# FFN output products that wait for the quarter of w_out they read, with scores one chunk further ahead

## The chip, the cores and the metric

One core of a Trainium2 chip runs the kernel. The metric is the device time of one execution in microseconds. The page and the trace come from one profiled execution.

## The reference

Talking-heads attention over 8 batches, 12 heads, 448 positions and 64 dimensions a head, then a feed-forward layer with a squared ReLU:

```python
scores = scale * np.matmul(q, k.transpose(0, 1, 3, 2))
scores = np.einsum('bhij,hg->bgij', scores, w_pre)
scores = scores - np.max(scores, axis=-1, keepdims=True)
attn = np.exp(scores)
attn = attn / (np.sum(attn, axis=-1, keepdims=True) + 1e-09)
attn = np.einsum('bhij,hg->bgij', attn, w_post)
out = np.matmul(attn, v)
# transposed to x: 3584 tokens x 768
h = np.maximum(x @ w_in, 0.0)      # w_in: 768 x 2048
result = (h * h) @ w_out           # w_out: 2048 x 768
```

Inputs and output are float32 in memory; the products are taken in bfloat16 with float32 sums.

## The kernel before

**A planner writes the order.** Every piece of work is given to a `Planner` as an operation with an engine (or a choice between DVE and ACT), a duration that the author estimated, a priority, and the operations that it depends on. `run()` plays the engines forward by these estimates: whenever an engine is free it takes the ready operation with the smallest priority. What comes out is one fixed order for each engine, in which the instructions are issued. The planner's dependences therefore decide only the order; on the chip, each instruction waits by semaphores for the data that it really reads and for the buffers that it overwrites, and an engine takes its instructions in order.

**Attention.** Work on a batch runs over 45 chunks of up to 10 query positions with all 12 heads (120 rows, plus 4 rows of padding). The place of a chunk, `n = 45 * b + c`, is the clock that all priorities count in. For a chunk:

- scores q·k for a whole block of positions (L741; four blocks a batch, `C0 = [0, 6, 19, 32]`), evacuated from PSUM to `snat` by DVE or ACT (`copy`, L534 and L536);
- a relayout by a DMA on SP's queue, `snat` to `sch` (`move`, called by `relayout`), so that heads lie on partitions;
- the mix of heads with w_pre on PE (L901, or L847 for two chunks at once on quarters of the array; L907 for the first chunks of batch 0), the row maximum on DVE (L912), the exponential on ACT (L915), the reciprocal on DVE (L922), w_post scaled by it on POOL (L925, tile `wq`);
- the mix with w_post, which also transposes (L932), evacuated into `atb` by DVE or ACT; then, for half a batch at once, the product with v (L978), evacuated into `xt`.

The scores of a block have the priority of the block's first chunk less `AHEAD`, less up to some nine chunks more for the earlier pairs of heads; a relayout has the priority of its chunk less `AHEAD`:

```python
pri = b * NCHUNK + first - AHEAD - 0.6 - (0.7 if r == 0 else 1.4) * (NPAIR - p)   # score
pri = n - AHEAD                                                                    # relayout
```

From batch 2 on, k and q are turned by DMA transposes on SP's queue (`x_piece`, `x_tail`), which stand between the relayouts there.

**FFN.** The tokens of two batches (896) are cut into units of 128 or 256 tokens; there are 17, numbered `ix`. A unit does its up products (L1037, `w1` against `xt`), a ReLU by DVE or ACT (L1051, L1055, tile `hr`), a square on POOL (L1058, tile `h2`), and its output products (L1076, `h2` against `w2`). All FFN products have priorities of a million and more, so PE takes them only where no attention work is ready: they are its filler. An output group is 128 tokens by 384 columns: 16 products over `ft`, planned in eight steps of two (`OSTEP = 2`, `f0 = 0, 2, ..., 14`).

**w_out** comes in four quarters on POOL's DMA queue, issued at steps 14, 17, 20 and 23 of batch 0 (`load_w2`, L1186). Quarter `f4` holds rows `f` from `8 * (f4 % 2)` (in units of 128) and columns from `384 * (f4 // 2)`: 0 and 1 are the first half of the columns, 2 and 3 the second half. `w2_in[f4]` is the planner's mark that it is there.

**Stand-ins.** Up to 130 us of planned time, where the planner finds PE without work and sparsely used, it puts in a product of a zero tile that nobody reads (`stand`, L1301, tile `still`), which keeps PE occupied.

Of the kernel before, what the change touches and what calls it, by code (L numbers as in the profile page):

```python
# [40 lines left out]
PIECE = NPAIR // 2  # L41
NE = 6
NSCH = 14
AHEAD = 7.0
FIFO = 50
IDLE_NS, IDLE_COLS, IDLE_FROM, IDLE_END, IDLE_LOW = 112, 256, 1300, 130000, 0.62
SPELL, PHASE, DROP, RISE = 3413, 1700, 0.4, 0.8
# [9 lines left out]
OSTEP = 2  # L57
# [28 lines left out]
SOON = 0  # L86
# [42 lines left out]
class Planner:  # L129
# [8 lines left out]
    def add(self, eng, ns, pri, fn, deps=(), lat=60, bank=None, frees=None, mode=0):  # L138
        op = Op(eng if isinstance(eng, dict) else {eng: ns}, lat, pri, fn, list(deps), bank, frees, mode)
        self.ops.append(op)  # L140
        return op
# [199 lines left out]
def kernel(  # L341
# [190 lines left out]
    def copy(eng, out_, in_):  # L532
        if eng == "DVE":
            nc.vector.tensor_copy(out=out_, in_=in_)  # L534
        else:
            nc.scalar.copy(out=out_, in_=in_)  # L536
# [4 lines left out]
    add = pl.add  # L541
    FILL = 1e6
    slots = {}
# [12 lines left out]
    def keep(key, fn):  # L556
        def go(*got):
            for key_, slot in zip(key if isinstance(key, list) else [key], got):
                slots[key_] = slot
            fn(*got)  # L560
        return go
# [12 lines left out]
    h_op, sq_op, o_op, st_op = {}, {}, {}, {}  # L574
# [137 lines left out]
    def place_of(b, c):  # L712
        return b * NCHUNK + (ORDER0.index(c) if b == 0 else c)
# [6 lines left out]
    def is_direct(b, c):  # L720
        return b == 0 and C0[1] <= c <= C0[2]
# [5 lines left out]
    def score(b, r, group):  # L727
# [17 lines left out]
        first = min(place_of(b, c) for c in range(C0[r], (C0 + [NCHUNK])[r + 1]) if not is_direct(b, c)) - b * NCHUNK  # L745
        pri = b * NCHUNK + first - AHEAD - 0.6 - (0.7 if r == 0 else 1.4) * (NPAIR - p)
        n = b * (NJ + 1) + r - 2
# [30 lines left out]
    def relayout(b, c):  # L778
# [6 lines left out]
        deps = list(scopy[b, r]) + (list(scopy[b, r - 1]) if r == 1 and cc == 0 else [])  # L785
        pri = n - AHEAD
        if r == 2 and cc == 0:
# [15 lines left out]
        else:  # L803
            o = cc - 1
            if b >= PAIR_FROM:
                pri = n - o % (2 * PAIRS) + 0.1 * (o % (2 * PAIRS)) - AHEAD
            o, step = (2 * CI * (o // 2) + o % 2, 2) if b >= PAIR_FROM else (o, CPR)
# [207 lines left out]
    def units_of(pair):  # L1015
        return UNITS if pair else UNITS0
# [3 lines left out]
    def unit(pair, ui):  # L1020
        a, z = units_of(pair)[ui]
        w = z - a
        nf = 512 // w
        ix = len(units)
        units.append((pair, ui))
        h2_ = h2[ix % 2]
        fill = FILL + 100 * ix
        xdeps = [op for t0, t1, op in xc_op[pair] if t0 < z and t1 > a]
        old_o = o_op.get(ix - 2, [])
        h_op[pair, a], sq_op[ix], o_op[ix] = [], [], []  # L1030
        prev = None
        for f0 in range(0, FT, nf):
            key = ("f", ix, "h", f0)
            for j in range(nf):
                def mms(slot, f0=f0, j=j):
                    for c2 in range(NPAIR):
                        nc.tensor.matmul(  # L1037
                            slot[:, j * w:(j + 1) * w], lhsT=w1[c2][:, (f0 + j) * 128:(f0 + j + 1) * 128],
                            rhs=xt[:, c2, a:z], start=(c2 == 0), stop=(c2 == NPAIR - 1),
                        )  # L1040
                if j == 0:
                    prev = add("PE", w * 2.55, fill + f0, keep(key, mms), xdeps + w1_in + [prev], lat=0, bank=key)
                else:
                    prev = add("PE", w * 2.55, 0, lambda key=key, mms=mms: mms(slots[key]), [prev], lat=0)
                h_op[pair, a].append(prev)
            end = add("WAIT%s" % str(key), 0, 0, lambda: None, [prev], lat=200)
            gi = len(hr_log)

            def relu(eng, key=key, gi=gi):
                if eng == "DVE":  # L1050
                    nc.vector.tensor_scalar(  # L1051
                        out=hr[gi % 2][:, :], in0=slots[key][:, :], scalar1=0.0, scalar2=0.0, op0=ALU.max, op1=ALU.add,
                    )
                else:
                    nc.scalar.activation(out=hr[gi % 2][:, :], in_=slots[key][:, :], func=ACT.Relu)  # L1055

            def square(gi=gi, f0=f0):
                nc.gpsimd.tensor_tensor(  # L1058
                    out=h2_[:, f0:f0 + nf, 0:w],
                    in0=hr[gi % 2][:, :].rearrange("p (f c) -> p f c", f=nf),  # L1060
                    in1=hr[gi % 2][:, :].rearrange("p (f c) -> p f c", f=nf), op=ALU.mult,
                )

            rl = add({"ACT": 500, "DVE": 590}, 0, 0, relu, [end, hr_log[gi - 2] if gi >= 2 else None], lat=100, frees=key)
            sq = add("POOL", 1020, FILL, square, [rl] + old_o, lat=70)
            hr_log.append(sq)
            sq_op[ix].append(sq)
        for mt in range(w // 128):
            whole = not (z == W2B and mt == 1 and pair == B // 2 - 1)
            cuts = [0, 384, DMODEL] if whole else [0, 384, 640, DMODEL]  # L1070
            for nt, (c0, c1) in enumerate(zip(cuts, cuts[1:])):
                key = ("f", ix, "o", mt, nt)
                for f0 in range(0, FT, OSTEP):
                    def mms(slot, f0=f0, mt=mt, c0=c0, c1=c1):
                        for ft in range(f0, f0 + OSTEP):
                            nc.tensor.matmul(  # L1076
                                slot[:, 0:c1 - c0], lhsT=h2_[:, ft, mt * 128:(mt + 1) * 128],
                                rhs=w2[:, ft, c0:c1],
                                start=(ft == 0), stop=(ft == FT - 1),
                            )  # L1080
                    if f0 == 0:
                        prev = add("PE", (12 + (c1 - c0) * 5 // 3) * OSTEP / 4, fill + 20 + 4 * mt + 2 * nt, keep(key, mms),
                                   [prev] + sq_op[ix][0:max(1, OSTEP // nf)] + w2_in[0:1 if ix < SOON else 4], lat=0, bank=key)
                    else:
                        prev = add("PE", (12 + (c1 - c0) * 5 // 3) * OSTEP / 4, FILL, lambda key=key, mms=mms: mms(slots[key]), [prev, w2_in[f0 // 4]] + sq_op[ix][0:(f0 + OSTEP + nf - 1) // nf], lat=0)
                    o_op[ix].append(prev)
                end = add("WAIT%s" % str(key), 0, 0, lambda: None, [prev], lat=200)
                si = ix_store[0]

                def evac(eng, key=key, si=si, c0=c0, c1=c1):  # L1090
                    copy(eng, osb[si % 2][:, c0:c1], slots[key][:, 0:c1 - c0])

                ev = add({"DVE": 80 + (c1 - c0) * 25 // 24, "ACT": 165 + (c1 - c0) * 5 // 7}, 0, 0, evac, [end, st_op.get(si - 2)] + ([m_op[n_] for n_ in direct] if si < 2 else []), lat=100, frees=key)
                evs = evs + [ev] if nt == 1 and whole else [ev]
                if nt == 1 or not whole:
                    done = []
                    for rows, dst, o in pieces(pair, a + mt * 128, None if whole else (c0, c1)):
                        side_ = not whole and rows <= CI
                        def store(dst=dst, o=o, rows=rows, si=si, e0=0 if whole else c0, e1=DMODEL if whole else c1, eng=nc.scalar if side_ else nc.gpsimd if whole else nc.sync):
                            eng.dma_start(out=dst, in_=osb[si % 2][o:o + rows, e0:e1])  # L1100
                        done.append(add("ACT" if side_ else "POOL" if whole else "SP", 510 if rows <= CI else 830 if whole else 930, FILL, store, evs))
                    for op in done:
                        op.store = whole
                    st_op[si] = pl.moved("LOAD" if whole else "DMA", 64, 16, 16, 0, done, 700)
            if whole:
                ix_store[0] += 1
# [70 lines left out]
    w2_in = [add("W2", 0, 0, lambda: None, lat=0) for i in range(4)]  # L1177
# [32 lines left out]
    def first_batch():  # L1210
# [35 lines left out]
        for gs in ONE:  # L1246
            av(0, 1, gs, P_ROWS, XB)
        unit(0, 2)

    def next_batch(b):  # L1250
# [91 lines left out]
```

## Time and profile before

| | |
|---|---|
| median of 3 runs | 571.62 us (571.61 to 571.78) |
| the profiled execution | 571.9 us, its span 570.1 us |
| PE busy | 561.1 us, 6340 products |
| DVE, ACT, POOL busy | 500.8, 446.4, 363.0 us |
| stand-in products (L1301) | 50 |
| output products (L1076) | 912, the first at 82.85 us |
| mean granted clock of PE | 0.999 |

The page gives busy time by engine, a strip of 40 slices of the span with busy shares in tenths, the chain of work that ended last, and groups of instructions by source line. Products on PE are pipelined, so the duration of one (323 ns for L1076) is longer than the distance between the starts of two. Times within the span count from its start.

### The profile page before, as it was taken

Reading aid. Unit: us, or ns where it says so; the run is one execution under the profiler, and the core shown is the slowest. Engines: PE = TensorE matmul, PEld = TensorE weight load, DVE = VectorE, ACT = ScalarE, POOL = GpSimd, SP = SyncE. Lnnn points to the kernel's source line nnn. Section 1 sums busy time; section 2 is a strip of 40 time slices with the busy share of each in tenths; the row PEclk is TensorE's granted clock in tenths of the full one; section 3 lists DMA queues with packets and bytes.
Section 4 is the critical chain, followed back from the end, with each engine's and each line's share of the span. In section 5 each row is a group of like instructions: output and inputs, shape, how many; then the busy total and the mean of one; then the engine's idle time right before and its main releaser. Section 6 shows DMA issues by size and latency. Waiting matters only on the chain.

```text
span 570.1 us, 17924 instructions
## 1 busy us (share of the span) xinstructions
PE 561.1 (98%) x6340; PEld 398.5 (70%) x6340; DVE 500.8 (88%) x1109; ACT 446.4 (78%) x1186; POOL 363.0 (64%) x677
## 2 busy tenths in 40 slices
PE   8999999999999999999999999999999999999997
PEld 5667765776677767677667677767667677767785
DVE  7999999999999899989888899998899998998542
ACT  5789988788788888888887888987888878888400
POOL 8667346776677448857578456957569554736451
PEclk9999999999999999999999999999999999999999
DMA  9999859974896739964797739975399656542011
GB/s 136 210 177 223 162 122 184 189 146 111 154 208 120 166 101 178 189 149 113 125 213 122 166 101 160 195 163 138 65 208 171 143 139 113 119 103 79 1 56 55
DMA packets 129949, 80.85 MB, mean 142 GB/s; under 512 B 59274, under 2 KB 126588, under 8 KB 129860
## 3 DMA queue, kind: packets, MB, share of 16 engines
q1 hardware_dynamic: 80756, 46.29, 37.0%
q0 software_dynamic: 49104, 33.43, 36.2%
q8 instruction: 49, 0.80, 0.6%
q14 instruction: 40, 0.33, 0.2%
HBM read 45.61 MB, written 11.01 MB: 99 GB/s over the span
## 4 chain that ended last, share of the span: by engine, by line
PE 90%; DVE 6%; POOL 1%; DMA 1%; issue 1%; ACT 0%; DVEq 0%; POOLq 0%; ACTq 0%
PE bank L1076 27%; PE bank L1037 25%; PE bank L932 13%; PE bank L741 7%; PE bank L978 7%; PE bank L847 5%; PE bank L901 3%; PE bank L907 2%; DVE mn L912 1%; DVE snat L534 1%; DMA sch<-snat 1%; DVE atb L534 1%; PE bank L1301 1%; DVE hr L1051 1%; DVE osb L890 1%
## 5 line engine op out<-in xcount | busy, mean ns | idle before, releaser
L915 ACT ACTIVATE es<-bank,mn 124x448 bf16<-124x448 f32 (+1 forms) x360 | 228.1, 642 | 42.9 <-DVE mn L912 35.8
L912 DVE TENSOR_REDUCE mn<-bank 124x1 f32<-124x448 f32 (+1 forms) x360 | 209.4, 613 | 3.9 <-PE bank L847 3.4
L1076 PE MATMUL bank<-w,h 128*128 128x384 bf16 (+2 forms) x912 | 177.3, 323 | 0.2
L1037 PE MATMUL bank<-xt,w 128*128 128x256 bf16 (+1 forms) x1632 | 164.1, 254 | 0.6 <-DVE hr L1051 0.3
L1037 PEld LDWEIGHTS <-w 128*128 128x128 bf16 x1632 | 132.8, 98 | 25.8 <-issue 12.2
L925 POOL TENSOR_SCALAR wq<-wback_two,rc 124x120 bf16<-124x120 f32 x252 | 88.8, 362 | 86.3 <-DVE rc L922 60.2
L1058 POOL TENSOR_TENSOR h<-hr 128x512 bf16<-128x512 f32 x112 | 115.7, 1037 | 33.1 <-DVE hr L1051 15.1
L932 PEld LDWEIGHTS <-es 124*112 124x112 bf16 (+2 forms) x1440 | 108.0, 129 | 32.5 <-issue 8.8
L534 DVE CAST atb<-bank 112x480 bf16<-112x480 f32 (+3 forms) x196 | 119.1, 617 | 10.6 <-PE bank L932 9.6
L932 PE MATMUL bank<-wq,es 124*112 124x120 bf16 (+2 forms) x1440 | 120.2, 217 | 2.0 <-POOL wq L925 1.5
L1076 PEld LDWEIGHTS <-h 128*128 128x128 bf16 x912 | 80.2, 98 | 55.0 <-issue 16.1
L536 ACT CAST atb<-bank 112x480 bf16<-112x480 f32 (+3 forms) x187 | 98.2, 539 | 16.1 <-PE bank L932 14.5
L536 ACT CAST snat<-bank 128x448 bf16<-128x448 f32 x168 | 84.6, 543 | 11.4 <-PE bank L741 10.6
L534 DVE CAST snat<-bank 128x448 bf16<-128x448 f32 x150 | 89.8, 614 | 0.8 <-PE bank L741 0.3
L1051 DVE TENSOR_SCALAR hr<-bank 128x512 f32<-128x512 f32 x82 | 56.6, 690 | 21.1 <-PE bank L1037 15.7
L915 ACT ACTIVATION_READ_ACCUMULATOR es<-bank,mn 124x1 f32 (+1 forms) x360 | 75.0, 208 | 0.0
L925 POOL TENSOR_SCALAR wq<-wback,rc 124x120 bf16<-124x120 f32 (+1 forms) x94 | 33.6, 365 | 39.3 <-DVE rc L922 26.1
L741 PE MATMUL bank<-kt,qz 64*64 64x448 bf16 (+1 forms) x528 | 44.6, 361 | 0.1
L847 PE MATMUL bank<-sch,wmix 64*64 64x448 bf16 x504 | 42.7, 363 | 0.0
L978 PE MATMUL bank<-atb,vs 112*64 112x192 bf16 (+3 forms) x864 | 40.4, 250 | 0.2 <-DVE atb L534 0.2
L978 PEld LDWEIGHTS <-vs 112*64 112x64 bf16 x864 | 36.5, 110 | 5.0 <-issue 4.5
L1100 POOL DMA_DIRECT2D out_dram<-osb x33 | 19.9, 604 | 29.9 <-DVE osb L534 16.4
(80 smaller groups left out, 397.7 us busy)
## 6 DMA issues: line engine op xcount, KB each, us to landing
sch<-snat SPq DMA_DIRECT2D x318, 105.0 KB
out_dram<-osb POOLq DMA_DIRECT2D x21, 384.0 KB, 3.8
vs<-in_v_dram POOLq DMA_DIRECT2D x16, 336.0 KB, 7.8
ks<-in_k_dram POOLq DMA_DIRECT2D x14, 336.0 KB, 8.0
qs<-in_q_dram POOLq DMA_DIRECT2D x14, 288.0 KB, 8.4
w<-in_moe_w_in_dram POOLq DMA_DIRECT2D x6, 512.0 KB, 13.0
w<-in_moe_w_out_dram POOLq DMA_DIRECT2D x4, 768.0 KB, 21.1
out_dram<-osb POOLq DMA_DIRECT2D x8, 192.0 KB, 7.5
```

Of the source, the lines that this page charges most:

```text
L534: nc.vector.tensor_copy(out=out_, in_=in_)
L536: nc.scalar.copy(out=out_, in_=in_)
L741: nc.tensor.matmul(slot[m0:m1, 0:S], lhsT=lhsT[:, m0:m1], rhs=kt[i][half, :, at_, :], start=True, stop=True,)
L847: nc.tensor.matmul(got[i + x][o0:o1, 0:S], lhsT=w[k0:k1, c0:c0 + o1 - o0], rhs=srcs[i + y][k0:k1, :], start=True, stop=True,)
L912: nc.vector.tensor_reduce(out=mn[i][0:rows, :], in_=slots[mk][0:rows, 0:S], axis=AX.X, op=ALU.min)
L915: nc.scalar.activation(out=es[i][0:rows, 0:S], in_=slots[mk][0:rows, 0:S], func=ACT.Exp, scale=-1.0, bias=mn[i][0:rows, 0:1], accum_out=sm ...
L925: nc.gpsimd.tensor_scalar(out=wq[i][0:rows, :, 0:ns], in0=back[0:rows, :, 0:ns], scalar1=rc[i // 2][0:rows, i % 2:i % 2 + 1], scalar2=1.0, ...
L932: nc.tensor.matmul(slot[0:P_KEYS, jb * H * ns:(jb + 1) * H * ns], lhsT=es[i][0:rows, jb * P_KEYS:(jb + 1) * P_KEYS], rhs=wq[i][0:rows, :, ...
L978: nc.tensor.matmul(v_[64 * hh:64 * hh + 64, i, 0:x1 - x0], lhsT=vs[:, 2 * c2 + hh, jb, :], rhs=atb[half][:, jb, 2 * c2 + hh, x0:x1], start ...
L1037: nc.tensor.matmul(slot[:, j * w:(j + 1) * w], lhsT=w1[c2][:, (f0 + j) * 128:(f0 + j + 1) * 128], rhs=xt[:, c2, a:z], start=(c2 == 0), sto ...
L1058: nc.gpsimd.tensor_tensor(out=h2_[:, f0:f0 + nf, 0:w], in0=hr[gi % 2][:, :].rearrange("p (f c) -> p f c", f=nf), in1=hr[gi % 2][:, :].rear ...
L1076: nc.tensor.matmul(slot[:, 0:c1 - c0], lhsT=h2_[:, ft, mt * 128:(mt + 1) * 128], rhs=w2[:, ft, c0:c1], start=(ft == 0), stop=(ft == FT - 1),)
```

## The change

One constant and the dependences of the output products. A group's first step no longer depends on all four marks, but on the mark of the quarter with its first rows and its columns; a later step depends on the quarter that it reads (`2 * (c0 // 384) + f0 // 8`) in place of `f0 // 4`. `AHEAD` goes from 7 to 8, which moves the priority of all scores and relayouts by one chunk. Nothing is computed in another way; the planner makes a new order for every engine from it.

```diff
-AHEAD = 7.0
+AHEAD = 8.0
...
                     if f0 == 0:
                         prev = add("PE", (12 + (c1 - c0) * 5 // 3) * OSTEP / 4, fill + 20 + 4 * mt + 2 * nt, keep(key, mms),
-                                   [prev] + sq_op[ix][0:max(1, OSTEP // nf)] + w2_in[0:1 if ix < SOON else 4], lat=0, bank=key)
+                                   [prev, w2_in[2 * (c0 // 384)]] + sq_op[ix][0:max(1, OSTEP // nf)], lat=0, bank=key)
                     else:
-                        prev = add("PE", (12 + (c1 - c0) * 5 // 3) * OSTEP / 4, FILL, lambda key=key, mms=mms: mms(slots[key]), [prev, w2_in[f0 // 4]] + sq_op[ix][0:(f0 + OSTEP + nf - 1) // nf], lat=0)
+                        prev = add("PE", (12 + (c1 - c0) * 5 // 3) * OSTEP / 4, FILL, lambda key=key, mms=mms: mms(slots[key]), [prev, w2_in[2 * (c0 // 384) + f0 // 8]] + sq_op[ix][0:(f0 + OSTEP + nf - 1) // nf], lat=0)
```

`SOON` is 0, so the first step before waits for `w2_in[0:4]` in every unit.

## The prediction

> **What bounds the kernel now.** The profile page first, for which engine sets the end.
>
> ```profile
> span 570.1 us, 17924 instructions
> PE 561.1 (98%) x6340; PEld 398.5 (70%) x6340; DVE 500.8 (88%) x1109; ACT 446.4 (78%) x1186; POOL 363.0 (64%) x677
> ...
> PE   8999999999999999999999999999999999999997
> ...
> DVE  7999999999999899989888899998899998998542
> ...
> PEclk9999999999999999999999999999999999999999
> ...
> PE 90%; DVE 6%; POOL 1%; DMA 1%; issue 1%; ACT 0%; DVEq 0%; POOLq 0%; ACTq 0%
> ```
>
> PE is busy in all slices and makes 90% of the chain that ended last; the clock granted is full. So the time is PE's own work plus what PE loses. A busy PE need not be useful, though: the timeline of PE, around the time at which the FFN output products begin, shows a hole.
>
> ```profile
> 76.18 0.80 PE L932 MATMUL bank<-wq,es 124*112 124x120 bf16 x8
> 76.81 0.73 PE L901 MATMUL bank<-sch,wmix 124*128 124x448 bf16 x3
> 77.38 1.91 PE L1301 MATMUL bank<-still 128*128 128x256 bf16 x16
> 80.41 0.37 PE L932 MATMUL bank<-wq,es 124*112 124x120 bf16 x4 [1.12 <-POOL wq L925]
> ...
> 82.85 0.49 PE L1076 MATMUL bank<-w,h 128*128 128x384 bf16 x2
> ```
>
> L1301 is the stand-in product whose result nobody reads. From 77.38 to 80.41 PE does nothing useful: 3.03 us, 1.91 in stand-ins and 1.12 idle. The first output product (L1076) starts only at 82.85. When its weights were there, the tile view of moe_w_out tells:
>
> ```profile
> L1186 POOL DMA_DIRECT2D w<-in_moe_w_out_dram x4: 922/928/939, 40.3 to 51.0; - x4
> DMA to landing us min/median/max: 16.4/21.1/25.1
> ```
>
> Issues at 40.3, 43.3, 48.3 and 51.0; landings by the trace's records at 56.7, 63.5, 70.3 and 76.1. The first quarter lay there for 26 us unread. What else limited PE in that stretch, the table of windows shows (columns: window, length, busy time of PE, PEld, DVE, ACT, POOL, clock, DMA):
>
> ```profile
> 60.00:70.00 10.00, 9.34 (x154) 7.28 (x149) 9.71 (x24) 9.35 (x28) 3.10 (x7) 1.00 0.77 153
> 70.00:77.00 7.00, 6.99 (x104) 5.21 (x102) 6.46 (x14) 6.36 (x16) 5.15 (x10) 1.00 0.68 154
> 77.00:81.00 4.00, 2.88 (x31) 2.17 (x29) 4.00 (x11) 3.12 (x10) 0.70 (x2) 1.00 0.34 76
> ...
> 336.00:346.00 10.00, 10.00 (x99) 6.49 (x91) 9.29 (x21) 9.57 (x25) 3.59 (x9) 1.00 0.35 79
> ```
>
> In 77 to 81 DVE is busy for 4.00 of 4.00: with FFN work exhausted, attention runs at DVE's pace and PE waits. In 336 to 346, in the middle of the kernel, PE is full.
>
> **Prices.** From the starts in the timeline of PE:
>
> ```profile
> 339.03 2.76 PE L1076 MATMUL bank<-w,h 128*128 128x384 bf16 x16
> 341.63 0.38 PE L932 MATMUL bank<-wq,es 124*112 124x120 bf16 x4
> 341.94 0.57 PE L741 MATMUL bank<-kt,qz 64*64 64x448 bf16 x8
> 342.44 0.42 PE L932 MATMUL bank<-wq,es 124*112 124x120 bf16 x4
> 342.69 0.49 PE L1076 MATMUL bank<-w,h 128*128 128x384 bf16 x2
> ```
>
> L1076: (341.63 − 339.03)/16 = 0.162 us each. L932 inside its group: 0.052 each by the trace, so four take 0.21; ahead of the quarter-array L741 they take 0.31, so a change of the array's tiling costs 0.10 at most (0.093 over all such places). A stand-in is 0.109. Priced this way over PE's whole order, the program before has 545.4 us of PE work; the other 24.7 us of the span are PE's start (1.06), its tail after the last product (3.4), the half-speed first microseconds, waits up to about 90 us (some 5), and rounding of the prices.
>
> **The change part by part.**
>
> *The wait for w_out.* Before, the first product of every output group is planned behind all four quarters (w2_in[0:4]); the later index f0 // 4 therefore never matters. After, columns 0 to 383 wait for quarter 0, then 1 from f0 = 8, and columns from 384 for 2 and 3. Only units 0 and 1 can notice, since later units are computed with all quarters landed. In the changed program's order, the first L1076 stands behind 28 chunks of L932 (before: 46). It needs quarter 0 after 28 chunks, 1 after 34, 2 after 41 and 3 after 44; the profile of before finishes those chunks at 58.1, 65.5, 76.3 and 81.4, so the landings leave 1.4, 2.0, 6.0 and 5.3 us. POOL issues the four loads behind the same counts of L925 (16, 18, 22, 24), so the landings should stay. The order holds 33 stand-ins in place of 50, and the run of sixteen at 77.38 is gone: output products stand there. Hole filled: −3.03 us; one more stand-in less: −0.1. Since PE is the bound to the end (27 us of pure FFN close the kernel), what is done early is missing from the end.
>
> *AHEAD 7 to 8.* Scores (L741), their evacuations and the relayouts (L772) get a priority one chunk earlier. Counts do not change: SP has 404 rows in both orders, the same 30 transposes among them, each up to four relayouts earlier or six later; nothing waits on SP that did not before. Seven changes of PE's tiling fewer (354 to 347): 7 × 0.093 = −0.65. Work moves from DVE to ACT: 16 L932 evacuations at 617 ns and 6 of scores at 614 leave DVE, 6 of osb at 548 and 5 relus at 690 come, together with 2 fewer xt some −8 us of DVE's 500.8; ACT gets about as much on its 446.4. Neither bounds the whole, so 0, and a help where DVE is full.
>
> *New tight places.* An order in which a consumer stands too close behind its producer stalls PE. I measured distances in PE work in both orders. From a mix (L847, L901) to the L932 of the same chunk, before has four below the 3.7 us at which the trace stops showing waits (short by 1.4 together; one of them gives the 0.31 us wait at 308.3), after has one (0.2). From an L932 to the next user of its bank or of its result, the shortest harmless distance is 0.95; before is short by 0.4 in all, after by 1.5 (eight places, the worst 0.53 at 47 us of PE work). Banks of mixes: before short by about 1.5 near 31 us of work, after by 0.8 there and 0.9 later. Sums 3.3 and 3.4; without the part of before that lies in the hole (0.5), after is worse by 0.6. Bounds: −2 (the early waits of before do not return) and +7.4 (second rival). I take +0.6, the counted value.
>
> Sum: −3.03 − 0.1 − 0.65 + 0.6 = −3.2 on the profiled execution's 571.9, so 568.7; the median of the runs lies 0.3 below that execution: **568.4**. Anything within 0.2%, 1.1 us, would pass for no change.
>
> The clock: the first seventeen stand-ins start 0.224 us apart, the sixteen at 77.38 run in 1.91 us, 0.119 each, and PEclk is full, so the hole cost no clock. The Trainium skill, "TensorE: Matmul & The Clock Gate", Part 1, speaks against removing stand-ins: it says that PE falls to half rate after an idle window of about 3.4 us. By that rule the sum would stay, because real products replace them; it would matter only in the third rival.
>
> **The rivals.**
>
> *The hole moves.* FFN products done early are missing later. By PE work, the new order has two stretches without any FFN product and with the earlier unit used up: 4.1 us at 101 to 105 (unit 2 done, unit 3 not begun) and 5.4 at 195 to 201 (unit 5 to 6). For it: the table above, where attention alone loses PE time: 60 to 81 us has 19.21 busy, less 1.91 of stand-ins, 17.3 useful of 21, 3.7 us lost. Against it: before has a like stretch, 4.1 us between units 9 and 10 near 346, and PE is 10.00 of 10.00 busy there. If one of the two stretches pays 3.0 to 3.7, the time is 571.4 to 572.1: no change.
>
> *Both stretches starve*, at the price of that early window: +7.4, 568.4 + 7.4 = 575.8. It ends slower than now by over 0.2% once the two together lose more than 3.2 + 1.1 = 4.3 us. Its place is attention at DVE's pace with one chunk more of score evacuations ahead of the row maxima. Against it: DVE has 8 us less to do.
>
> *A quarter lands late.* PE takes its queue in order, so an L1076 waiting for quarter 0 or 1 holds L932 and L901 of the following chunks, and with them POOL, DVE and ACT. Margin 1.4 us; relayouts a chunk earlier share the DMA engines (0.77 busy in 60 to 70). Each us of lateness beyond it costs one us. If a wait of 4 us also put PE back to the pace of its first stand-ins for as long as those lasted (3.81 us, half of it lost), the time is 568.4 + 4.0 + 1.9 = 574.3. Without the clock it needs 4.3 us of wait to be slower.
>
> That the edit does nothing is excluded by the two orders.
>
> **How the numbers follow.** Forecast 0.66, one stretch starves 0.15, both 0.11, late quarter 0.08. Faster 0.67 (the forecast and a sliver of the second), same 0.14, slower 0.19. The forecast's own range is 565.8 (early waits of before gone, −2.6) to 570.4; the range reaches on over the one-stretch case to 573.0.
>
> **What would show it.** Right: 33 stand-ins, none near 77; first L1076 near 59 us with no idle naming the w_out load ahead of it; PE over 9.8 of 10 in 60 to 70 and full from 70 to 90; DVE about 493 busy; span near 566.9. Wrong: PE idle with wq or mn as releaser near 110 to 120 or 210 to 218 us (the stretches), an L1076 waiting for DMA (late quarter), PEclk below 9 in an inner slice, or PE busy unchanged at 561 with the stand-ins gone, which would mean that the prices, not the waits, moved.

## The result: slower by 0.9%, where 0.6% faster was forecast

The changed kernel takes 576.48 us in the median (575.11 to 578.54, five runs) against 571.61 us for the kernel before (571.54 to 571.78): ratio 1.0091, 95% interval 1.0067 to 1.0115. The forecast was 568.4 with a range up to 573.0. The profiled execution took 576.48 us, so it is 4.6 us longer than that of before, and 7.8 us longer than the sum of the prediction. The runs of the changed kernel differ with the clock that they were granted: 575.1 us at a mean of 0.999, 578.5 at 0.994.

The page of the changed kernel, the lines that were shown of before:

```profile
span 574.5 us, 17927 instructions
PE 561.0 (98%) x6323; PEld 396.7 (69%) x6323; DVE 495.4 (86%) x1096; ACT 452.4 (79%) x1199; POOL 365.3 (64%) x677
...
PE   8999999979999999999999999999999999999997
...
PEclk9999999989999999999999999999999999999999
...
PE 85%; DVE 7%; DMA 3%; issue 2%; ACT 2%; POOL 1%; DVEq 0%; POOLq 0%; ACTq 0%
```

In the ninth slice (115 to 129 us) PE is busy for 7 tenths at 8 tenths of its clock, and 3% of the last chain is now DMA, all of it relayouts (`sch<-snat`). PE's busy time has not fallen although 17 stand-ins are gone.

The part of the change that the prediction priced with confidence came out as written. The timeline of PE at the first output products, and at the place of the old hole:

```profile
58.97 0.35 PE L901 MATMUL bank<-sch,wmix 100*128 100x448 bf16 x1
59.41 0.49 PE L1076 MATMUL bank<-w,h 128*128 128x384 bf16 x2
...
77.10 0.49 PE L1076 MATMUL bank<-w,h 128*128 128x384 bf16 x2
77.43 0.38 PE L932 MATMUL bank<-wq,es 124*112 124x120 bf16 x4
77.64 0.93 PE L901 MATMUL bank<-sch,wmix 124*128 124x448 bf16 x4
```

The first L1076 starts at 59.41 (before 82.85) with no wait for its load, and products of FFN stand where stand-ins stood. The four loads landed at 53.1, 59.7, 66.5 and 73.3, 3 to 4 us earlier than in the kernel before, so the margin was wider than the prediction took. The table of windows says the same (columns: window, length, busy time of PE, PEld, DVE, ACT, POOL, clock, DMA), and goes on to where the time went:

```profile
60.00:70.00 10.00, 9.80 (x134) 6.45 (x134) 9.54 (x23) 8.82 (x24) 2.50 (x8) 1.00 0.77 152
70.00:77.00 7.00, 7.00 (x117) 5.57 (x116) 6.61 (x15) 6.14 (x17) 4.04 (x8) 1.00 0.47 126
77.00:81.00 4.00, 4.00 (x47) 3.03 (x47) 4.00 (x10) 3.59 (x10) 1.52 (x3) 1.00 0.13 18
118.00:130.00 12.00, 9.01 (x82) 6.90 (x80) 7.63 (x17) 6.91 (x19) 6.31 (x12) 0.86 0.72 149
...
220.00:240.00 20.00, 19.23 (x217) 14.68 (x213) 19.37 (x43) 17.01 (x45) 18.34 (x30) 1.00 1.14 180
```

From 118 to 130 us PE is busy for 9.01 of 12.00 at a clock of 0.86 (the kernel before: 12.00 of 12.00 at 1.00). The timeline of PE there:

```profile
118.73 1.48 PE L1037 MATMUL bank<-xt,w 128*128 128x256 bf16 x12
120.13 0.35 PE L741 MATMUL bank<-kt,zt 128*128 128x448 bf16 x1
123.47 0.35 PE L901 MATMUL bank<-sch,wmix 124*128 124x448 bf16 x1 [2.99 <-DMA sch<-snat]
123.66 0.54 PE L741 MATMUL bank<-kt,zt 128*128 128x448 bf16 x2
124.04 0.72 PE L932 MATMUL bank<-wq,es 124*112 124x120 bf16 x8
124.56 2.77 PE L1037 MATMUL bank<-xt,w 128*128 128x256 bf16 x12
```

A mix stands 2.99 us idle for its relayout, and behind it the clock is halved: twelve up products take 2.77 us, where twelve took 1.48 just before. PE takes its queue in order, so the up products behind the mix, whose data lay ready, stood too. What stood ahead of the relayout, the issues on SP's queue tell (changed kernel first, then before):

```profile
106.02 2.49 SPq L643 DMA_TRANSPOSE zt<-qt  x1
108.62 4.64 SPq L673 DMA_TRANSPOSE kt<-kn  x1
113.36 4.11 SPq L679 DMA_TRANSPOSE qz<-qn  x1
117.52 12.95 SPq L772 DMA_DIRECT2D sch<-snat  x14
```

```profile
104.93 4.29 SPq L673 DMA_TRANSPOSE kt<-kn  x1
109.34 1.38 SPq L643 DMA_TRANSPOSE zt<-qt  x1
110.81 1.38 SPq L679 DMA_TRANSPOSE qz<-qn  x1
112.24 11.83 SPq L772 DMA_DIRECT2D sch<-snat  x12
```

Three transposes of batch 2 hold SP for 11.24 us (2.49 + 4.64 + 4.11) in place of 7.05, so the relayouts behind them start at 117.52 and not at 112.24. The chain of waits has the one that the mix stood for as 5.00 us of DMA from 118.34. The same `qz` transpose took 1.38 us in one kernel and 4.11 in the other.

**A ledger.** With the prices of the prediction, every product on PE has a start that PE's work alone would give it. What the real start lies behind that is what PE has lost so far. Read at five times, in the two profiled executions (us):

| | PE work | lost 0–60 | 60–100 | 100–200 | 200–240 | 240–end |
|---|---|---|---|---|---|---|
| before | 545.4 | 9.1 | 3.9 | 1.8 | 0.9 | 5.8 |
| changed | 542.9 | 9.7 | 1.5 | 8.2 | 3.2 | 5.7 |
| difference | −2.5 | +0.6 | −2.4 | +6.4 | +2.3 | −0.1 |

The differences add up to +4.3; the span grew by 4.4. The hole and the counted work brought about what was forecast, and 8.7 us came back between 100 and 240 us. Read in steps of 10 us, some 4.8 of these lie at 120 to 130; 0.9 at 150 to 160, where a second mix waits 0.73 us for its relayout (at 159.73); 1.5 at 230 to 240, where both attention and FFN are there and DVE is full; the rest is spread. Work at half pace counts as lost, too: a clock of 0.86 over 12 us is 1.7 us of full pace, within the 4.8.

Two rows of the changed kernel say where the loss at 200 to 240 us is and where it is not:

```profile
205.00:215.00 10.00, 10.00 (x100) 4.88 (x98) 9.62 (x22) 9.29 (x26) 3.36 (x9) 1.00 0.42 91
230.00:234.00 4.00, 3.39 (x37) 2.58 (x36) 4.00 (x9) 3.45 (x11) 3.42 (x6) 1.00 1.46 214
```

From 215.2 to 221.2, between the last output product of FFN unit 5 and the first up product of unit 6, attention is alone on PE. By the same prices that stretch holds 5.4 us of PE work, and 0.6 us is lost in it.

### The profile page after: what moved, and what is told of

Same layout as the page of the kernel before. It is cut to its first block, busy times and chain, and to the rows that moved or that the text cites. A ratio compares the mean times of both kernels' runs of the same rounds, so it can differ in the third digit from the quotient of the medians.

```text
span 574.5 us, 17927 instructions
## 1 busy us (share of the span) xinstructions
PE 561.0 (98%) x6323; PEld 396.7 (69%) x6323; DVE 495.4 (86%) x1096; ACT 452.4 (79%) x1199; POOL 365.3 (64%) x677
## 4 chain that ended last, share of the span: by engine, by line
PE 85%; DVE 7%; DMA 3%; issue 2%; ACT 2%; POOL 1%; DVEq 0%; POOLq 0%; ACTq 0%
PE bank L1037 25%; PE bank L1076 24%; PE bank L932 13%; PE bank L741 7%; PE bank L978 6%; PE bank L847 5%; DMA sch<-snat 3%; PE bank L901 3%; DVE mn L912 2%; ACT es L915 1%; PE bank L907 1%; POOL wq L925 1%; DVE atb L534 1%; DVE hr L1051 1%; PE bank L1301 1%
## 5 line engine op out<-in xcount | busy, mean ns | idle before, releaser
L1076 PE MATMUL bank<-w,h 128*128 128x384 bf16 (+2 forms) x912 | 181.0, 324 | 0.2
L536 ACT CAST atb<-bank 112x480 bf16<-112x480 f32 (+3 forms) x203 | 105.3, 533 | 24.7 <-PE bank L932 23.8
L932 PE MATMUL bank<-wq,es 124*112 124x120 bf16 (+2 forms) x1440 | 122.0, 218 | 1.8 <-POOL wq L925 1.0
L534 DVE CAST atb<-bank 112x480 bf16<-112x480 f32 (+2 forms) x180 | 111.4, 628 | 10.6 <-PE bank L932 9.8
L1076 PEld LDWEIGHTS <-h 128*128 128x128 bf16 x912 | 79.8, 98 | 54.3 <-issue 16.3
L536 ACT CAST snat<-bank 128x448 bf16<-128x448 f32 x174 | 88.2, 545 | 9.9 <-PE bank L741 8.9
L534 DVE CAST snat<-bank 128x448 bf16<-128x448 f32 x144 | 85.7, 613 | 4.3 <-DMA sch<-snat 2.2
L1051 DVE TENSOR_SCALAR hr<-bank 128x512 f32<-128x512 f32 x87 | 59.9, 689 | 23.1 <-PE bank L1037 19.3
L847 PE MATMUL bank<-sch,wmix 64*64 64x448 bf16 x504 | 41.3, 362 | 0.7 <-DMA sch<-snat 0.7
```

The lines of the kernel that those rows point to most:

```text
L847: nc.tensor.matmul(got[i + x][o0:o1, 0:S], lhsT=w[k0:k1, c0:c0 + o1 - o0], rhs=srcs[i + y][k0:k1, :], start=True, stop=True,)
L932: nc.tensor.matmul(slot[0:P_KEYS, jb * H * ns:(jb + 1) * H * ns], lhsT=es[i][0:rows, jb * P_KEYS:(jb + 1) * P_KEYS], rhs=wq[i][0:rows, :, ...
L1076: nc.tensor.matmul(slot[:, 0:c1 - c0], lhsT=h2_[:, ft, mt * 128:(mt + 1) * 128], rhs=w2[:, ft, c0:c1], start=(ft == 0), stop=(ft == FT - 1),)
```

## The experiments

The theories, by the letters that the expectations use: A, the late second half of batch 2 (its k load waits for a later POOL issue, and its transposes and relayouts with it) makes the wait at 120 us; B, `AHEAD = 8` is the harm by itself; C, FFN products done early are missing later; D, the copies `kn`, `qn` on POOL come behind the squares of an FFN unit that now starts earlier; E, any other order of the same work loses, because the planner does not foresee the waits. All ratios are against the kernel before, run on the same chip, with the 95% interval.

### Each half of the change alone

`w2_only` has the new w_out waits and the old constant, `ahead_only` the reverse:

```diff
# w2_only: the changed kernel with
-AHEAD = 8.0
+AHEAD = 7.0
# ahead_only: the kernel before with
-AHEAD = 7.0
+AHEAD = 8.0
```

> The changed kernel with AHEAD back at 7: only the waits for w_out are changed. The changed kernel's trace shows one wait of 3.0 us at 120.1 to 123.5 for a relayout, queued on SP behind three transposes that took 2.5, 4.6 and 4.1 us, while a k load of batch 2 that POOL issued late (behind 62 L925 in place of 53) was landing. In this program the k load stands behind 53 again. Theory A (the late k load and what it holds up costs the time): no wait near 120, and the gains of the prediction appear, 567.5 to 569.5 us. Theory B (AHEAD 8 crowds SP and DVE all along): the same, 567.5 to 569.5, so this run alone does not part A from B. Theory C (FFN products done early leave a stretch without FFN work later, in which attention runs at DVE's pace): 571 to 573 us, with PE below 4.8 of 5 in windows near 215 to 237.

> The kernel before with AHEAD at 8: the waits for w_out stay at all four quarters. The k load stands behind 53 L925. Theory A (late k load): no wait of 3 us near 120, 570 to 572.5 us, with the hole near 77 still there. Theory B (AHEAD 8 crowds SP and DVE): 574 to 577 us. Theory C: about 571.6, since the FFN products start as late as before.

Measured: `w2_only` 572.06 us (571.08 to 575.56), ratio 1.0009 [0.9995, 1.0023]: no change. `ahead_only` 580.24 (579.22 to 581.6), 1.0149 [1.0131, 1.0167]. The constant costs 8.6 us alone and 4.4 on top of the other edit; the w_out waits bring nothing by themselves, though their hole is filled (loss at 60 to 100 us: 1.3). In `w2_only`, 3.7 us more than before are lost at 200 to 240 us, up to 1.7 of them at half pace (the clock of 0.83 in its row for 205 to 215 below). So C's range holds for `w2_only`, with the loss at 207 to 218 and not at 215 to 237; `ahead_only` lies above all three ranges. `ahead_only` loses its time elsewhere than the changed kernel; its PE at 115 us:

```profile
114.97 0.38 PE L847 MATMUL bank<-sch,wmix 64*64 64x448 bf16 x3
117.54 0.90 PE L847 MATMUL bank<-sch,wmix 60*60 60x448 bf16 x5 [2.19 <-issue]
```

Here, too, the mix comes late behind a `kt` transpose on SP (issued at 112.98, the relayout behind it at 115.60), though the profile names no releaser, and here, too, PE runs at half pace after it: 9.0 us are lost at 100 to 200. The clock is 0.51 from 117 to 124 us, and that alone is 3.4 of the 9.0.

### The wait at 120 us

`k_free` takes the late k load out of the planner's limit of seven loads (in the changed kernel it is issued at 107.1 us, before at 92.3); `stand_in` leaves the wait and fills it with 24 stand-ins, which ask for no data, so that the clock stays up:

```diff
# k_free: the changed kernel with
-        if len(loads) >= 7:
+        if len(loads) >= 7 and len(loads) != 25:
# stand_in: the changed kernel with, ahead of the mix of chunk 77,
+            if n == 77:
+                for _ in range(24):
+                    stand(slot, 0)
```

> The changed kernel, both edits, with one planner dependence left out: the second k load of batch 2 no longer waits for the load seven loads before it (a v load that slipped behind an output store). Its issue returns from behind 62 L925 to behind 53. Theory A: the wait at 120 goes with its half-speed clock after it, 570.5 to 572.5 us if only the 4.9 us that PE lost there come back, and a clock of 0.999 in every run. Theory B: still a wait for a relayout near 120, 574 us or more. Theory C: 571 to 573, with the loss near 216 to 237 left.

> The changed kernel with 24 stand-in products (2.6 us) put into PE's queue right ahead of the mix that waits at 120 us; they wait for nothing but their bank. The wait for the relayout stays. If the spread of the changed kernel's runs (575.1 to 578.5, clock 0.999 to 0.994) is PE's clock halved after an idle time of 3 us, every run shows a clock of 0.999 and 574.5 to 575.7 us. If the spread comes from the DMA side (how long the transposes take), it stays as wide, 575 to 578.5.

`k_free`: 577.02 us (576.66 to 578.4), 1.0095 [1.0078, 1.0112]. The wait at 120 is gone (2.1 us lost at 100 to 200, the changed kernel 8.2). That does not prove A: of the second half's transposes that of k is issued no earlier (134.67; in the changed kernel 134.56) and only that of q is (137.50 for 141.46), and the first half's hold SP as long (106.20 to 117.01). So transposes that hold SP until 117 us do not make the wait by themselves; PE has to come to such a mix by then, and in the planner's new order it does not. A's and C's ranges are missed, and B's is met without B's wait. The time is the same, because 5.9 us are lost at 200 to 240 in place of 3.2, with this line of PE's timeline in the middle:

```profile
208.43 0.42 PE L847 MATMUL bank<-sch,wmix 64*64 64x448 bf16 x4
211.54 0.72 PE L932 MATMUL bank<-wq,es 124*112 124x120 bf16 x8 [2.69 <-POOL wq L925]
```

`stand_in`: 575.22 us (574.32 to 576.93), 1.0062 [1.0045, 1.0079]. PE is full and at full clock from 118 to 130:

```profile
118.00:130.00 12.00, 12.00 (x129) 10.04 (x130) 9.23 (x21) 8.88 (x24) 7.64 (x15) 1.00 0.76 151
```

The median falls by 1.3 us and the profiled execution by 2.2, about the 1.7 of half pace; but the runs of the two kernels overlap, so the size is not settled. They were to lie at 574.5 to 575.7 with the clock at 0.999 in every run, and they spread from 574.32 to 576.93 with 0.994 in the slowest: the halved clock at this place is not all of the spread. The wait itself stays, now filled with work that nobody reads. So a busy PE at full clock can still be late.

### The place at 205 to 215 us

FFN unit 5 takes the first 128 tokens of batch 2, which the first half of that batch's attention gives; unit 6 needs the second half. Between them PE has attention alone. Three kernels ask what makes that stretch dear. `w2_half` gives DVE less to do in batch 2 (its row maxima run over 224 of 448 keys: another constant is subtracted before the exponential, and the normalized result stays the same but for rounding); the `near` kernels let the POOL copies go ahead of the FFN squares, with a control on the kernel before:

```diff
# w2_half: w2_only with
-in_=slots[mk][0:rows, 0:S]
+in_=slots[mk][0:rows, 0:S // 2 if b == 2 else S]
# w2_near, before_near, after_near: w2_only, the kernel before, the changed kernel with
-NEAR_LAST = 2e6
+NEAR_LAST = 9e5
```

> The w_out waits alone, with DVE lightened in batch 2 only: the row maximum there is taken over half of the keys (224 of 448), so that L912 falls from 613 to about 390 ns for 45 chunks, 10 us of DVE's time. (A softmax doesn't depend on which constant is subtracted.) The planner knows nothing of it, so the order is the same as in the run with the w_out waits alone. Theory C (attention at DVE's pace starves PE in 205 to 215): the loss of 3.8 us in 200 to 220 falls under 1.5, 568.5 to 570 us. Theory D: less than that, since attention has fallen behind by late scores and not by DVE: 570 to 572 us.

> The w_out waits alone (AHEAD 7), and POOL's copies of k and q (L660) planned ahead of the FFN squares (NEAR_LAST from 2e6 to 9e5, where squares have 1e6). In the run with the w_out waits alone, up products start 7 us earlier than before (115.2 for 122.2), their squares take POOL, and the copies for the second half of batch 2 run at 123 to 135 in place of 118 to 122; its second pair of transposes is issued at 133 and 136 in place of 124 and 126. Theory D (the early FFN products delay batch 2 through POOL, PE spends its FFN work meanwhile, and starves when that is used up, near 207): transposes back near 124 to 127, DVE over 18.5 of 20 in 140 to 160, the gap between units 5 and 6 under 5 us, and 568 to 570 us. Theory C alone (FFN work is missing later whatever POOL does, since attention is held by DVE): the gap stays over 8 us and the time 571 to 573.

> The control to the run with the copies first: the kernel before with the same NEAR_LAST, nothing else. Its copies for batch 2 stand where they stood (behind 72 to 74 L925), so theory D expects 570.5 to 572.5 us, with the hole of 3 us near 77 still there. If the order of the copies were worth something by itself, it would be faster by as much as the run with the w_out waits.

> The changed kernel with the copies first (both edits and NEAR_LAST 9e5). Its copies for the second half of batch 2 move from behind 76 to 86 L925 to behind 74 to 78. Theory D: part of the loss between 130 and 240 us goes; the wait at 120 us, which comes from the first pair of transposes, may stay: 571 to 574 us. Theory B (AHEAD 8 by itself): 575 or more.

`w2_half`: 571.61 us (570.6 to 574.65), 1.0010 [0.9995, 1.0026]; the loss at 200 to 240 falls from 4.6 to 3.4, where C asked for under 1.5 and 568.5 to 570 us. The rows of `w2_only` and of `w2_half`:

```profile
205.00:215.00 10.00, 8.75 (x80) 5.52 (x81) 9.42 (x21) 9.97 (x28) 3.40 (x9) 0.83 0.40 108
```

```profile
205.00:215.00 10.00, 8.65 (x105) 5.87 (x103) 9.51 (x22) 9.97 (x28) 3.41 (x9) 1.00 0.42 112
```

The longest wait for `wq` there is 0.96 us in place of 1.00, and the clock was not halved this time, which alone can be the 1.2 us. So it is not shown that DVE's row maxima are a part of the price; ACT is as good as full (9.97 of 10) in both kernels. `w2_near`: 578.21, 1.0118 [1.0097, 1.014]; `before_near`: 579.97, 1.0138 [1.0115, 1.0161]; `after_near`: 585.46, 1.0239 [1.0214, 1.0265]. In `w2_near` unit 6 follows unit 5 after 0.8 us in place of 10.3 and the loss at 200 to 240 is 1.8; but the control shows that the edit costs 8 us by itself (3.6 us are lost at 440 to 460, where nothing of this change happens). `after_near` loses 9.7 at 100 to 200. D is not settled by these kernels: the gap closes, at a price that hides what closing it is worth, and all three times lie above D's ranges.

`before_6` makes attention later instead of FFN earlier, with the old w_out waits; `w2_75` is the new waits with half the step:

```diff
# before_6: the kernel before with
-AHEAD = 7.0
+AHEAD = 6.0
# w2_75: the changed kernel with
-AHEAD = 8.0
+AHEAD = 7.5
```

> The kernel before with AHEAD = 6.0 in place of 7.0: attention work admitted one mix later, the step of ahead_only in the other direction, w_out waits as they were. Theory B (harm grows with AHEAD): not slower than before, 569 to 572. Theory E (any re-planned order loses): 574 to 580 us, with waits over 1 us at batch starts. Theory F (7.0 is the middle, later attention starves the softmax instead): slower too, but the loss lies where attention is at DVE's pace (DVE over 9.8 of 10 in the slice that grows), not at a relayout or a w_out wait.

> The new w_out waits with AHEAD = 7.5, half of the change's step. Theory B: between 572.06 (7.0) and 576.5 (8.0), near 574, the loss near 117 to 131 us appearing in part. Theory E: anywhere from 571 to 580, not ordered by AHEAD; which waits appear is not a part of those of 8.0. Faster than both, under 571, if an order between the two keeps the 3 us of the hole and meets neither loss.

`before_6`: 579.75 us (579.45 to 580.78), 1.0149 [1.0134, 1.0164], so B's "not slower" is wrong: one mix later costs as much as one earlier. The time is in E's range; F's sign, DVE full where the loss is, is missing (1.61 and 0.99 of 2 us in the windows 212 to 214 and 214 to 216). Its PE loses 4.2 us at 200 to 240, at the same place and for the same releaser as `k_free`, without the w_out edit (and some 5 us more than the kernel before after 240):

```profile
211.91 0.38 PE L741 MATMUL bank<-kt,qz 64*64 64x448 bf16 x4
214.76 0.70 PE L932 MATMUL bank<-wq,es 124*112 124x120 bf16 x8 [2.47 <-POOL wq L925]
```

`w2_75`: 573.9 (572.51 to 574.32), 1.0039 [1.0024, 1.0054], between the two as B asked, but with none of the loss near 120 that B asked for (2.2 us at 100 to 200) and 4.2 at 200 to 240.

### Four variants in three orders

If the order as such decides (E), then a change that means nothing should move the time too. `TURN` is the planner's price for a change of PE's tiling; 92 or 98 ns in place of 95 moves its sum by 1 us and gives another order of the same work:

```diff
-TURN = 95
+TURN = 98     # before_turn, w2_turn, ah_t98, af_t98; and 92 in before_t92, w2_t92, ah_t92, af_t92
```

> The kernel before, w_out waits and AHEAD 7.0 as they were, with one price of the planner moved by 3 ns: TURN, what it reckons for a change of the PE array's tiling, 98 in place of 95. No work is added, removed or allowed earlier; only the planner's sums differ, by 1.0 us over 354 changes, and with them the order it settles on (23,513 lines of PE's order differ; 337 changes of tiling in place of 354, -1.6 us at 0.093 each). Theory E (the order of the kernel before is one that happens to fit the chip, and any other order of the same work meets waits of 1 to 3 us that the planner does not see, at batch starts): 574 to 580 us, a few waits over 1 us at places where the kernel before has none, and the hole near 77 us still there. Theory B (AHEAD 8.0 is itself the harm: attention work admitted one mix earlier) : 570 to 572, no new waits over 1 us.

> The new w_out waits with AHEAD 7.0 and TURN = 98 in place of 95, the same 3 ns as in before_turn. With before_turn it makes a second pair for the w_out edit alone under another order. Theory E: w2_turn stands to before_turn as the 3 us of the hole make it, with a spread of some us: 571 to 579, and its loss is not at w2_only's 207 to 218. Theory C (what FFN work is done early is missing later, whatever the order): about equal to before_turn, a gap between FFN units 5 and 6 of 5 us or more.

> AHEAD 8.0 alone (old w_out waits), TURN 92 in place of 95: another order of the same plan. Theory B (AHEAD 8.0 as such is dear): 577 to 582 us, like ahead_only's 580.24, with several us lost between 100 and 140 us. Theory E (the order decides, not AHEAD): anywhere from 571 to 582, the losses at other places than ahead_only's.

> AHEAD 8.0 alone, TURN 98. Theory B: 577 to 582 us, several us lost between 100 and 140 us. Theory E: anywhere from 571 to 582, other places.

> Both edits (the changed kernel), TURN 92. Theory B with C (AHEAD 8.0 loses near 100 to 140 us, and FFN work done early is missing near 200 to 240 us): 575 to 579, with a loss at both places. Theory E: 571 to 580, waits elsewhere.

> Both edits, TURN 98. Theory B with C: 575 to 579, with a loss at both places. Theory E: 571 to 580, waits elsewhere; under 571 would make it the best version of all and the forecast's 568.4 reachable by order alone.

> The kernel before with TURN 92. Theory C with B (the w_out edit and AHEAD 8.0 lose, not the order): 570 to 573 us as at 95 and 98, the hole near 77 us still there and nothing over 1 us lost at 200 to 240 us. Theory E: anywhere from 571 to 580.

> The new w_out waits with AHEAD 7.0 and TURN 92. Theory C (FFN work done early is missing later): 571 to 578, with 2 to 5 us lost at 200 to 240 us beyond the kernel before's 0.9, as in all other kernels with these waits so far. Theory E: anywhere, from 568.5 (the hole's 3 us kept) to 578, the loss not bound to that place.

Median us, with the ratio's interval for the new ones:

| | TURN 92 | 95 | 98 | mean |
|---|---|---|---|---|
| before | 572.99 [1.0008, 1.005] | 571.6 | 572.73 [1.0016, 1.0055] | 572.4 |
| w_out waits | 575.64 [1.0049, 1.0107] | 572.06 | 577.73 [1.0093, 1.0145] | 575.1 |
| AHEAD 8 | 573.78 [1.0019, 1.0051] | 580.24 | 577.93 [1.0064, 1.0148] | 577.3 |
| both | 579.68 [1.0098, 1.0157] | 576.48 | 582.12 [1.0163, 1.0202] | 579.4 |

And the ledger of each profiled execution, with the time from the last output product of unit 5 to the first up product of unit 6:

| | PE work | 0–60 | 60–100 | 100–200 | 200–240 | 240–end | gap 5 to 6 |
|---|---|---|---|---|---|---|---|
| before 92 | 543.9 | 9.1 | 5.0 | 2.1 | 1.1 | 6.6 | 0.2 |
| before 95 | 545.4 | 9.1 | 3.9 | 1.8 | 0.9 | 5.8 | 0.8 |
| before 98 | 543.8 | 9.1 | 3.3 | 2.5 | 0.8 | 7.9 | 4.3 |
| w_out 92 | 543.0 | 9.1 | 1.1 | 4.7 | 5.6 | 6.3 | 13.3 |
| w_out 95 | 542.2 | 8.8 | 1.3 | 3.4 | 4.6 | 7.3 | 10.3 |
| w_out 98 | 543.6 | 8.9 | 0.6 | 6.5 | 5.3 | 8.3 | 13.2 |
| AHEAD 92 | 543.6 | 10.0 | 3.5 | 2.4 | 1.7 | 7.2 | 5.1 |
| AHEAD 95 | 543.3 | 9.6 | 4.0 | 9.0 | 1.5 | 7.7 | 0.2 |
| AHEAD 98 | 543.8 | 10.3 | 4.5 | 2.2 | 1.5 | 7.4 | 0.5 |
| both 92 | 543.7 | 10.0 | 1.4 | 8.0 | 4.5 | 6.8 | 9.9 |
| both 95 | 542.9 | 9.7 | 1.5 | 8.2 | 3.2 | 5.7 | 5.9 |
| both 98 | 544.0 | 10.1 | 1.7 | 4.4 | 8.3 | 8.4 | 13.1 |

The ledger holds half pace, too: about 1.7 us in before 92 (near 80 us), w_out 95, w_out 98 (near 215) and both 95 (near 125), and 3.4 in AHEAD 95.

Four things follow.

*C holds for the w_out waits, but not for the changed kernel's own order.* The six kernels with the new waits lose 2.8 us less at 60 to 100 on the mean (1.3 against 4.0), and 4.0 more at 200 to 240 (5.2 against 1.2): each of the six above 3.1, each of the six others below 1.8. In five of the six the loss sits in the gap. Counted inside the gap alone, gaps of up to 5.1 us lose at most 0.2 us, and gaps of 9.1 to 13.6 lose 2.4 to 5.4 (`w2_half`, `w2_75`, `k_free` and `before_6` among them, the last with the old waits). The changed kernel is the exception, with `stand_in`, which has its order: 0.6 lost in a gap of 5.9, and 1.4 of its 3.2 at 230 to 234. What a long gap is like, the windows 205 to 215 tell, of before (at 95) and of the w_out waits at 92:

```profile
205.00:215.00 10.00, 10.00 (x109) 6.74 (x109) 9.47 (x21) 9.16 (x26) 3.13 (x9) 1.00 0.38 87
```

```profile
205.00:215.00 10.00, 7.15 (x69) 3.88 (x67) 10.00 (x24) 9.52 (x29) 3.49 (x10) 1.00 0.56 162
```

In this kernel it looks like the hole of 77 us again, DVE busy for all of 10.00 and PE waiting, only later. In others it is not DVE that is full: in `w2_only` and `w2_half` it is ACT. So what is common is that attention alone does not fill PE; which engine holds it is not shown. And PE's timeline in the second kernel has the line that the prediction had set down as the sign of its first rival:

```profile
207.54 0.43 PE L847 MATMUL bank<-sch,wmix 64*64 64x448 bf16 x4
209.51 0.70 PE L932 MATMUL bank<-wq,es 124*112 124x120 bf16 x8 [1.54 <-POOL wq L925]
...
211.46 0.71 PE L932 MATMUL bank<-wq,es 124*112 124x120 bf16 x8 [0.87 <-POOL wq L925]
```

*The new waits are slower in five of the six pairs*, by 2.4 us on the mean of the six (+2.7, +0.5, +5.0 at AHEAD 7; +5.9, −3.8, +4.2 at 8). Values that spread so far do not show that the mean differs from nothing; what they show is no gain.

*AHEAD 8 is slower in all six pairs*, by 0.8 to 8.6 us, 4.6 on the mean; B holds as to the sign of this step, though `before_6` shows that the harm does not grow with `AHEAD`. (The 0.8, at TURN 92, is hardly more than those two medians can tell.) One part of it recurs in every order, 0.5 to 1.2 us before 60 us. PE's window 54 to 60, before and AHEAD 8, both at 92:

```profile
54.00:60.00 6.00, 5.94 (x97) 4.27 (x95) 5.76 (x16) 5.68 (x17) 3.12 (x7) 1.00 1.23 223
```

```profile
54.00:60.00 6.00, 5.42 (x86) 3.98 (x85) 5.45 (x16) 5.83 (x17) 2.44 (x5) 1.00 1.27 229
```

The rest has no fixed place: the 9.0 at 100 to 200 of `ahead_only` are 2.4 and 2.2 in its other two orders.

*E is half right.* The kernel before keeps its time within 1.4 us in three orders (571.6 to 573.0; `before_turn` lies below E's 574 to 580); but `before_6` and `before_near`, larger steps away from it, cost 8 us. The other three variants move by 5.6 to 6.5 us for 3 ns in a planner's constant, so their single runs against each other say little. A gap without FFN work does not explain all of that: `AHEAD` 8 alone has short gaps in all three orders and moves by 6.5 us, by a wait and half pace at 115 to 124 us in one of them. The expected ranges fared accordingly: B's time came for `ah_t98` without its place, and for `ah_t92` not at all; C's "about equal to `before_turn`" missed `w2_turn` by 5.0 us, though the gap was there; `w2_t92` came as C said in time and place; `af_t92` and `af_t98` lie above B with C, `af_t98` above E as well.

No kernel here beats the one before.

## Why the prediction was wrong, step by step

- **The step that failed: "nothing waits on SP that did not before", in "AHEAD 7 to 8", priced at 0.** In the changed kernel a mix waits 2.99 us for its relayout at 120 us, the relayout stands behind three transposes on SP that take 11.24 us in place of 7.05, and the clock is halved after it: some 4.8 us more lost at 120 to 130 than before, and 0.9 more at 150 to 160, where another mix waits for a relayout. (In `k_free` the transposes hold SP until 117 us too and no mix waits; so it is their length together with the place of the mix in PE's order.) The prediction compared the rows of SP's order by their number and place and not by their lengths, though the trace of before had `kt` at 4.29 us and `qz` at 1.38. The whole term is 4.4 us on top of the other edit, 0.9 of them before 60 us. Why transposes of one kind differ so in length stays open.
- **"New tight places", +0.6, was mis-sized with it.** The runs show +8.7 between 100 and 240 us. The term was found by distances in PE's order, and these do not contain SP's queue, nor DVE's, which is full at 230 to 234 us, where another 1.5 us went.
- **The wait for w_out** was right in its own place: 33 stand-ins and none near 77, first L1076 at 59.41, no wait for w_out, PE at 9.80 of 10 in 60 to 70 and full after, DVE at 495.4 (493 said). Predicted −3.0 to −3.1; the ledger shows −2.4 at 60 to 100, −2.8 on the mean of six pairs.
- **Seven changes of tiling fewer**: PE's work fell by 2.5 us as counted, stand-ins included. Right.
- **The first rival, the hole moves,** is not what slowed the changed kernel. Its two stretches are there as counted, 4.4 us long with 4.0 of PE work at 112.6 to 117.0, and 5.9 us long with 5.4 of work at 215.2 to 221.2; they lose 0.4 and 0.6 us. The argument against it, that PE was full in a like gap near 346, held for gaps of that size. With the w_out waits alone the gap is 10.3 us and loses 3.8, up to 1.7 of it at half pace, with `wq` as the releaser; that its price of 3.0 to 3.7 gave 571.4 to 572.1 and `w2_only` came to 572.06 is partly luck.
- **The second rival, both stretches starve, 575.8,** is closest in time to the 576.48 of the result (0.11 given), by luck: neither stretch starved in this kernel.
- **The clock**: the half pace of the third rival came due, though for a relayout and not for w_out, and for 1.7 us of full pace rather than 1.9. (Its 0.224 us for the first stand-ins is their 3.81 us divided by seventeen; their starts lie 0.21 apart.) The rule of the Trainium skill that the prediction cited, "TensorE: Matmul & The Clock Gate", Part 1, has the half rate after an idle window of about 3.4 us; here 2.99 us of idle time were enough.
- **The signs of being wrong**: PE's clock below 9 in an inner slice came, and so did PE busy at 561 with the stand-ins gone. The latter was to mean that prices moved; but PE's idle time rose by 4.5 us (9.0 to 13.5), and up to 1.7 us of its busy time is half pace.

What stays open: why the other 3.7 us that the mean of the pairs shows for `AHEAD = 8` turn up in another place in each order, which engine holds attention in the long gaps, and whether an order exists that fills the hole at 77 us and loses nothing after it.

## What to carry to other kernels

Filler work that is done early can be missing later: before you count a filled hole, find the stretch that this filler covered and read there, by windows, whether the other engines can feed PE without it. Here, between units 5 and 6, gaps of up to 5.9 us cost 0.6 us at most, gaps of 9 us and more 2.4 to 5.4. When a planner writes the order, two neighbouring edits cannot be told apart from one run each; move a constant that means nothing and see how far the time moves, and compare the edits over several such orders. And check the queue that carries the data (here SP's transposes and relayouts) for lengths, not for counts.

## What the runs showed of the hardware

- A DMA transpose holds SP's queue for very different times: the first `qz` of batch 2 1.38 us before and 4.11 in the changed kernel, its first `kt` 2.53 in `ahead_only` and 6.72 in `k_free`, the second 1.37 in the changed kernel and in `k_free`. What sets the length was not tried.
- The half clock does not need one long idle stretch. In `ahead_only` a wait of 2.19 us was followed by a clock of 0.51 from 117 to 124 us. In `w2_only` the longest wait near 210 us was 1.00 us, but PE was busy for only 1.14 and 1.60 of two windows of 2 us, and then ran at 0.50. In `k_free` 2.69 us of full idle left the clock at 1.00. These are the windows of `w2_only`, and then those of `k_free` around its wait:

```profile
208.00:210.00 2.00, 1.14 (x9) 0.51 (x9) 2.00 (x6) 2.00 (x7) 0.60 (x2) 1.00 0.36 51
210.00:212.00 2.00, 1.60 (x14) 1.15 (x14) 2.00 (x6) 2.00 (x8) 1.51 (x5) 0.74 0.82 265
212.00:214.00 2.00, 2.00 (x17) 1.46 (x17) 1.90 (x5) 2.00 (x6) 0.57 (x2) 0.50 0.53 151
```

```profile
208.00:210.00 2.00, 0.85 (x13) 0.37 (x6) 2.00 (x5) 0.94 (x4) 0.58 (x1) 1.00 0.42 159
210.00:212.00 2.00, 0.46 (x7) 0.39 (x7) 2.00 (x6) 2.00 (x7) 0.70 (x2) 1.00 0.37 80
212.00:214.00 2.00, 1.81 (x23) 1.11 (x23) 2.00 (x7) 1.53 (x6) 1.09 (x4) 1.00 0.55 150
```
